# Attention and MLP on one core: q and k of the first groups transposed in 128-wide PE steps into one PSUM bank, with few long dummy matmuls

## Chip, cores, metric

One core of one Trainium2 chip. The metric is the device time of the whole program in microseconds (us). A time is quoted as the median of several executions; a profiled execution shows a span that is about 1.8 us shorter than its time.

Names used below: PE is TensorE, PEld its weight load, DVE VectorE, ACT ScalarE, POOL GpSimd, SP SyncE. Sizes such as 64\*64 or 128\*64 in a line of PE are the rows and columns of its array that the instruction uses; the text calls this its tiling. A 128x64 step is also called half-width.

## The reference

```python
# q, k, v: (8 batches, 12 heads, 448, 64), float32
scores = q @ k.T / sqrt(64) - log(448)
attn = sigmoid(scores)                       # no softmax
x = (attn @ v) -> (8 * 448 tokens, 768)
h = x @ w_in                                 # 768 x 2048
out = gelu_tanh(h) @ w_out                   # 2048 x 768
```

The kernel computes in bf16 with float32 accumulation. It treats four heads as one "group": 3 groups to a batch, 24 in all, each of 7 "units".

## The kernel before

A small scheduler inside the program simulates the engines, decides the order of the instructions on each, and then writes out the waits. So an edit of one cost or one bank also moves instructions elsewhere. q and k of the first two batches (groups 0 to 5) are transposed on PE, later ones by DMA. The parts that matter:

```python
def make_warm():                     # dummies, meant to keep PE's clock up until q and k are there
    x, y = take_pair(plan.now)
    def fn(e):
        for _ in range(4):
            for a in range(2):
                rows = slice(64 * a, 64 * a + 64)
                r = mm(ps[0:64, (x, y)[a], 0:128], ident[rows, 0:64], ident[rows, :], start=True, stop=True)
# ...
def make_trans(t):                   # one of q, k of one group: 28 steps of 64x64, two banks
    x, y = take_pair(t)
    def fn(e):
        for j in range(NJ):          # NJ = 7
            for (a, c) in ((0, 0), (1, 1), (0, 1), (1, 0)):
                rows = slice(64 * a, 64 * a + 64)
                r = nc.tensor.transpose(ps[64*c:64*c+64, (x, y)[a], 32*j:32*j+32].bitcast(BF16),
                                        part[rows, j, c, :], ident[rows, rows])
# ... then one copy out of PSUM (DVE; for group 0 DVE and ACT share it)
# qk: 4 matmuls of 64x448 a unit, then a sigmoid on ACT (batch 0) or tanh on ACT and a scaling on DVE;
# av: 4 matmuls of 64x448 a unit; MLP: 6 matmuls a tile with w_in, gelu on ACT, 16 with w_out
EARLY = "v0 q2 v1 v2 q3 v3 w0 w1 q4 v4 w2 q5 v5 w3 o0 o1 o2 o3"   # order of the loads that POOL issues
```

In EARLY, q2 means "k and q of group 2", w0 to w3 the quarters of w_in, o0 to o3 those of w_out.

Of the kernel before, what the change touches and what calls it, by code (L numbers as in the profile page):

```python
# [12 lines left out]
BF16 = mybir.dt.bfloat16  # L13
# [29 lines left out]
        self.clock = None  # L43


class Plan:


# [32 lines left out]
        return True  # L81

    def begin(self, op, t):
        op.deps = [d() if callable(d) else d for d in op.deps]
        cost = op.cost
        if op.eng == "PE":
            t0 = t
            if op.mode != self.pe_mode and self.pe_mode is not None:
                t0 = t + self.SWITCH
            self.pe_mode = op.mode  # L90
            op.start = t0
            self.free["PE"] = t0 + cost
            op.end = t0 + cost + op.lat
        elif op.eng in QUEUES:
            op.start = t
            self.free[op.eng] = float("inf") if op.hold else t + cost
            if op.hold:
                self.blocker = op
            go = t + cost * 0.5 + self.DMA_HEAD[op.eng] + (0.0 if self.order[op.eng] else self.DMA_FIRST[op.eng])
            self.flow[op.eng].append([op, float(op.pkt[0]), go])  # L100
            heapq.heappush(self.events, go)
            self.dma_count[op.sem] = self.dma_count.get(op.sem, 0) + 16
            op.target = self.dma_count[op.sem]
        else:
            op.start = t
            self.free[op.eng] = t + cost
            op.end = t + op.lat
        op.pos = len(self.order[op.eng])
        self.order[op.eng].append(op)
        if op.end is not None:  # L110
            heapq.heappush(self.events, op.end)
        if self.free[op.eng] != float("inf"):
            heapq.heappush(self.events, self.free[op.eng])
# [153 lines left out]
def bass_sigmoid_attention__then__act_gelu_tanh_kernel(  # L267
# [8 lines left out]
    B, H, S, D = q.shape  # L276
    assert D == 64 and H % 4 == 0 and S % 64 == 0 and B % 2 == 0
    NJ = S // 64
    NG = H // 4
# [25 lines left out]
    with contextlib.ExitStack() as stack:  # L305
# [26 lines left out]
        def copy(e, o, i, who):  # L332
            if who == "ACT":
                return e.activation(o, i, AF.Copy)  # L334
            return e.tensor_copy(o, i)  # L335
# [23 lines left out]
        def take(t):  # L359
            ok = [i for i in range(NPS) if bank_ok(i, t)]  # L360
            lone = [i for i in ok if not bank_ok(i ^ 1, t)]
            i = (lone or ok)[0]
            bank_busy[i] = True
            return i

        def take_pair(t):
            i = [i for i in range(0, NPS, 2) if bank_ok(i, t) and bank_ok(i + 1, t)][0]
            bank_busy[i] = bank_busy[i + 1] = True
            return i, i + 1

        def free_pairs(t):
            return sum(1 for i in range(0, NPS, 2) if bank_ok(i, t) and bank_ok(i + 1, t))
# [4 lines left out]
        def give(i, op):  # L377
            bank_free[i] = op
            bank_busy[i] = False

        def make_warm():

            x, y = take_pair(plan.now)
            prev = [bank_free[x], bank_free[y]]

            def fn(e):
                r = None
                for _ in range(4):
                    for a in range(2):
                        rows = slice(64 * a, 64 * a + 64)  # L390
                        r = mm(ps[0:64, (x, y)[a], 0:128], ident[rows, 0:64], ident[rows, :],  # L391
                               start=True, stop=True)
                return r

            op = Op("warm", "PE", fn, [eye] + prev, 235.0 if plan.now > 5500.0 else 450.0, 165.0, mode=64)
            give(x, op)
            give(y, op)
            return op


        G = B * NG
        units = [(g, j) for g in range(G) for j in range(NJ)]
        cast_q, cast_k, tr_q, tr_k, ld_q, ld_k, ld_v = {}, {}, {}, {}, {}, {}, {}
        tr_too = []
        freed_q, freed_k = {}, {}
        qk, tanh, aff, av, evac = {}, {}, {}, {}, {}
        trans = []
# [14 lines left out]
        def low_load(nm, g):  # L422

            return 2 <= g < PE_TR * NG
# [80 lines left out]
                                               prio=(1, g), sem="tr%s%d" % (nm, st), pkt=(112, 26.0), hold=0.6))  # L505

        def trans_ready(t):
            if not trans or eye.end is None or eye.end > t or free_pairs(t) < 1:
                return False
            g, nm, src, dst, cast, tr, freed, after = trans[0]  # L510
            return g in cast and cast[g].end is not None and cast[g].end <= t

        def make_trans(t):
            g, nm, src, dst, cast, tr, freed, after = trans.pop(0)
            x, y = take_pair(t)
            prev = [bank_free[x], bank_free[y]]
            flat = src[:].rearrange("p j c d -> p (j c d)")
            part = flat.rearrange("p (j c d) -> p j c d", j=NJ, c=2) if not low_load(nm, g) else \
                flat.rearrange("p (c j d) -> p j c d", c=2, j=NJ)
            to = ps[:, x:y + 1, 0:NJ * 32].bitcast(BF16)  # L520

            def fn(e):
                r = None
                for j in range(NJ):
                    for (a, c) in ((0, 0), (1, 1), (0, 1), (1, 0)):
                        rows = slice(64 * a, 64 * a + 64)
                        r = nc.tensor.transpose(ps[64 * c:64 * c + 64, (x, y)[a], 32 * j:32 * j + 32].bitcast(BF16),
                                                part[rows, j, c, :], ident[rows, rows])
                return r

            freed[g] = op = Op("trp%s%d" % (nm, g), "PE", fn, [eye, cast[g]] + prev, NJ * 70.0, 165.0, mode=64)
            o = dst[:].rearrange("p j x -> p (j x)").rearrange("p (a y) -> p a y", a=2)
            if g == 0:
                two = [plan.add(Op("trc%s%d.%d" % (nm, g, a), w,
                                   lambda e, a=a, w=w: copy(e, o[:, a], to[:, a], w),
                                   [op], 330.0, 450.0, prio=(0, -1))) for a, w in ((0, "DVE"), (1, "ACT"))]
                tr[g] = two[0]
                tr_too.extend(two[1:])
                give(x, two[0])
                give(y, two[1])  # L540
                return op
            tr[g] = plan.add(Op("trc%s%d" % (nm, g), "ANY",
                                lambda e, who: copy(e, o, to, who),
                                [op] + after, 0, 0, prio=(0, g),
                                alts={"DVE": (560.0, 680.0)}))
            give(x, tr[g])
            give(y, tr[g])
            return op

        def by_half(t, g):  # L550

            if g < PE_TR * NG:
                return t[:].rearrange("p j x -> p (j x)").rearrange("p (a j r) -> p a j r", a=2, j=NJ)
            return t[:].rearrange("p j (a r) -> p a j r", a=2)

        def make_qk(n, t):
# [4 lines left out]
            x, y = take_pair(t)  # L561
            prev = [bank_free[x], bank_free[y]]
            both = ps[:, x:y + 1, 0:S]
            kv, qv = by_half(kT[s], g), by_half(qT[s], g)

            def fn(e):
                r = None
                for (a, c, half) in ((0, 0, 0), (0, 1, 1), (1, 1, 0), (1, 0, 1)):
# [3 lines left out]
                           start=True, stop=True)  # L572
                return r

            qk[(g, j)] = op = Op("qk%d.%d" % (g, j), "PE", fn, [tr_q[g], tr_k[g]] + (tr_too if g == 0 else []) + prev,
                                 4 * 2.5 + S / 2.4, 165.0, mode=64)
            pg, pj = units[n - NAT] if n >= NAT else (None, None)
            old = av[pg] if pg is not None else None
# [243 lines left out]
        def qk_ready(t, n):  # L822
            if n >= len(units):
                return False
            g, j = units[n]
            if g not in tr_q or n >= NAT and units[n - NAT][0] not in av:
                return False
            return all(d.end is not None and d.end <= t for d in [tr_q[g], tr_k[g]] + tr_too)

        def units_done(g, t):  # L830

# [35 lines left out]
        def pe_next(pl, t):  # L867
# [8 lines left out]
            go_a, go_b = a_ready(t), b_ready(t)  # L876
            mlp = go_a or go_b
            banks = free_banks(t)
            if trans_ready(t) and mlp:
                g, nm = trans[0][:2]  # L880
                both = [x for x in trans[:2] if x[0] == g]
                if free_pairs(t) >= len(both) and all(x[4][g].end is not None and x[4][g].end <= t for x in both):
                    ops = [make_trans(t) for x in both]
                    state["queue"] = ops[1:]
                    return ops[0]
            can = 0
            if n <= LEAD + UB * 0.5 * (a_prog + b_prog):
                while can < BURST and qk_ready(t, n + can):
# [4 lines left out]
            if not mlp:  # L893
                if can and left <= 1 and free_pairs(t) and banks >= (2 if av_open else 4):
                    op = make_qk(n, t)
                    state["n"] += 1
                    return op
                soon = trans_ready(t) and trans[0][0] <= units[min(n + 3, len(units) - 1)][0]
                if m and not soon:
                    return av_take(1, t)[0]  # L900
                return make_trans(t) if trans_ready(t) and free_pairs(t) >= (1 if soon or not 0 < n < UB else 2) else None
            whole = m > 0 and state["avj"] + m == NJ
            room = (banks - (2 if whole and not av_open else 0)) // 2
            size = min(can, room, free_pairs(t))
# [121 lines left out]
```

## Time and profile before

| | before |
|---|---|
| time, median of the first 3 runs | 396.77 us (395.6 to 396.88) |
| span of the profiled run, its mean granted clock | 394.7 us, 0.995 |
| PE busy | 382.2 us, 97% |
| chain that ended last | 86% PE |

Three parts of the page: the engines' busy time in 40 equal slices (about 10 us each; a digit is tenths), the granted clock of PE, and the shares of the chain that ended last.

```profile
PE   7779999999999999999999999999999999999996
ACT  5988974377779757777657666567657733333211
PEclk9989999999999999999999999999999999999999
DMA  8999999539698566588667548727211011111133
...
PE 86%; DMA 6%; ACT 4%; DVE 1%; SPq 1%; issue 1%; POOL 0%
```

Read: PE is full from the fourth slice to the end. Only the first three slices have room, and in the second and third ACT is fuller than PE (9 and 8 against 7). The third slice has a clock of 0.8.

The next fence is PE's timeline in that slice, then ACT's. Columns: start, time, engine, line, operation, output and inputs, sizes, count; in brackets the idle time before it and what ended it.

```profile
22.34 0.36 PE L617 MATMUL ps<-at,vb 64*64 64x448 bf16 x4
22.86 0.38 PE L527 MATMUL ps<-ident,qb 64*64 64x64 bf16 x22 [0.17 <-DVE kT L335]
25.10 0.25 PE L527 MATMUL ps<-ident,qb 64*64 64x64 bf16 x6 [1.86 <-issue]
25.16 0.38 PE L570 MATMUL ps<-qT,kT 64*64 64x448 bf16 x4
```

```profile
20.30 3.39 ACT L581 ACTIVATE at<-ps 128x896 bf16<-128x896 f32 x4
25.59 1.73 ACT L581 ACTIVATE at<-ps 128x896 bf16<-128x896 f32 x2 [1.89 <-PE ps L570]
```

In the middle of one transpose, after 22 of 28 equal steps whose data and banks were all there, PE stops for 1.86 us and the profile knows no releaser ("issue"). ACT, the busiest engine of this stage, then waits 1.89 us for the qk behind it. In the next fence the stretches of 1 us show PE's clock after that stop: the column after the engines' busy times is PEclk, the last two are the DMA share and GB/s.

```profile
23.00:24.00 1.00, 0.24 (x22) 0.13 (x17) 0.00 (x0) 0.69 (x1) 1.00 (x3) 1.00 1.22 197
24.00:25.00 1.00, 0.00 (x0) 0.00 (x0) 0.00 (x0) 0.00 (x0) 1.00 (x2) 1.00 1.25 202
...
27.00:28.00 1.00, 1.00 (x16) 0.22 (x8) 0.00 (x0) 1.00 (x2) 1.00 (x2) 0.50 1.26 201
```

### The profile page before, as it was taken

How to read it: one execution, taken by the hardware profiler on the slowest of the kernel's cores; microseconds unless marked ns; L12 is line 12 of the kernel's file. 1: busy time of each engine (PE TensorE's matmuls, PEld its weight loads, DVE VectorE, ACT ScalarE, POOL GpSimd, SP SyncE). 2: the span in 40 equal slices, each digit the busy share in tenths (PEclk: the TensorE clock that was granted, in tenths of full speed). 3: DMA queues.
4: the chain of work that ended last, by engine and by line, in shares of the span. 5: the costliest groups of instructions: out<-in, count | busy, mean ns of one | idle time of the engine just before them, and what ended most of it. 6: DMA issues, size and time to landing. Idle time of an engine off the chain costs nothing.

```text
span 394.7 us, 7961 instructions
## 1 busy us (share of the span) xinstructions
PE 382.2 (97%) x3456; PEld 199.1 (50%) x3456; DVE 134.7 (34%) x226; ACT 243.3 (62%) x382; POOL 51.2 (13%) x82
## 2 busy tenths in 40 slices
PE   7779999999999999999999999999999999999996
PEld 6324445555544554554554555545554555555563
DVE  3336633036546524554434443343333210000000
ACT  5988974377779757777657666567657733333211
POOL 6992110011102010201110101101000000000000
PEclk9989999999999999999999999999999999999999
DMA  8999999539698566588667548727211011111133
GB/s 237 192 200 204 210 213 319 89 72 184 172 206 193 135 128 163 141 181 178 164 132 177 138 77 169 174 64 181 65 40 42 0 42 42 40 40 42 40 81 80
DMA packets 63523, 51.77 MB, mean 131 GB/s; under 512 B 36224, under 2 KB 60032, under 8 KB 63488
## 3 DMA queue, kind: packets, MB, share of 16 engines
q1 hardware_dynamic: 48320, 36.61, 37.6%
q0 software_dynamic: 14528, 13.64, 21.9%
q10 hardware_dynamic: 640, 1.02, 0.7%
q8 instruction: 27, 0.44, 0.4%
q14 instruction: 8, 0.07, 0.0%
HBM read 45.61 MB, written 11.01 MB: 143 GB/s over the span
## 4 chain that ended last, share of the span: by engine, by line
PE 86%; DMA 6%; ACT 4%; DVE 1%; SPq 1%; issue 1%; POOL 0%
PE ps L721 35%; PE ps L662 34%; PE ps L570 8%; PE ps L617 7%; DMA qf<-in_q_dram 4%; ACT at L581 3%; DMA vb<-in_v_dram 1%; DMA kf<-in_k_dram 1%; ACT th L589 1%; DVE at L593 1%; SPq L755 1%; ACT gT L694 0%; PE ps L676 0%; DVE qb L335 0%; DVE kT L335 0%
## 5 line engine op out<-in xcount | busy, mean ns | idle before, releaser
L662 PE MATMUL ps<-xT,w_in 128*128 128x448 bf16 x762 | 154.4, 353 | 0.4 <-DVE kT L335 0.2
L721 PE MATMUL ps<-w_out,gT 128*128 128x384 bf16 x896 | 153.1, 326 | 0.0
L593 DVE TENSOR_SCALAR at<-th 128x896 bf16<-128x896 f32 x147 | 92.4, 628 | 140.6 <-ACT th L589 140.1
L589 ACT ACTIVATE th<-ps 128x896 f32<-128x896 f32 x147 | 129.1, 927 | 1.0 <-PE ps L570 1.0
L721 PEld LDWEIGHTS ps<-w_out,gT 128*128 128x128 bf16 x896 | 86.2, 98 | 63.3 <-ACT th L589 2.9
L662 PEld LDWEIGHTS ps<-xT,w_in 128*128 128x128 bf16 x762 | 71.1, 98 | 76.7 <-ACT th L589 3.9
L694 ACT ACTIVATE gT<-ps 128x448 bf16<-128x448 f32 x128 | 71.2, 556 | 43.2 <-PE ps L662 43.2
L334 ACT ACTIVATE ob<-ps 128x384 f32<-128x384 f32 x56 | 27.5, 490 | 95.4 <-PE ps L721 95.4
L570 PE MATMUL ps<-qT,kT 64*64 64x448 bf16 x672 | 47.7, 362 | 3.8 <-ACT at L581 2.9
L466 POOL DMA_DIRECT2D vb<-in_v_dram x24 | 14.8, 617 | 217.4 <-PE ps L570 214.5
L617 PE MATMUL ps<-at,vb 64*64 64x448 bf16 x672 | 39.8, 353 | 0.8 <-DMA vb<-in_v_dram 0.8
L570 PEld LDWEIGHTS ps<-qT,kT 64*64 64x64 bf16 x672 | 14.8, 105 | 31.5 <-issue 15.9
L617 PEld LDWEIGHTS ps<-at,vb 64*64 64x64 bf16 x672 | 19.8, 107 | 12.0 <-DMA vb<-in_v_dram 1.1
L335 DVE CAST xT<-ps 128x448 bf16<-128x448 f32 x26 | 15.8, 619 | 11.7 <-PE ps L617 11.7
L581 ACT ACTIVATE at<-ps 128x896 bf16<-128x896 f32 x21 | 17.3, 949 | 2.7 <-PE ps L570 2.7
L335 DVE CAST kb<-kf 128x896 bf16<-128x896 f32 (+1 forms) x21 | 13.1, 623 | 14.2 <-DMA kf<-in_k_dram 14.2
L468 POOL DMA_DIRECT2D vb<-in_v_dram x24 | 17.6, 733 | 0.2 <-issue 0.2
L335 DVE CAST qb<-qf 128x896 bf16<-128x896 f32 x19 | 11.9, 625 | 9.8 <-DMA qf<-in_q_dram 9.8
L334 ACT ACTIVATE xT<-ps 128x448 bf16<-128x448 f32 x22 | 12.2, 560 | 2.5 <-PE ps L617 2.3
L776 POOL DMA_DIRECT2D w_in<-in_moe_w_in_dram x16 | 9.9, 652 | 0.0
L391 PE MATMUL ps<-ident 64*64 64x128 bf16 x112 | 5.5, 277 | 1.8 <-POOL ident L342 1.5
L391 PEld LDWEIGHTS ps<-ident 64*64 64x64 bf16 x112 | 5.1, 150 | 1.9 <-POOL ident L342 1.5
(27 smaller groups left out, 33.8 us busy)
## 6 DMA issues: line engine op xcount, KB each, us to landing
out_dram<-ob SPq DMA_DIRECT2D x54, 192.0 KB, 2.7
kf<-in_k_dram SPq DMA_DIRECT2D x19, 448.0 KB, 4.6
qf<-in_q_dram SPq DMA_DIRECT2D x18, 448.0 KB, 5.6
vb<-in_v_dram POOLq DMA_DIRECT2D x48, 112.0 KB, 5.2
w_in<-in_moe_w_in_dram POOLq DMA_DIRECT2D x16, 192.0 KB, 10.9
w_out<-in_moe_w_out_dram POOLq DMA_DIRECT2D x4, 768.0 KB, 22.3
kb<-in_k_dram POOLq DMA_DIRECT2D x4, 224.0 KB, 8.9
qb<-in_q_dram POOLq DMA_DIRECT2D x4, 224.0 KB, 9.4
```

The source lines that it names most:

```text
L334: return e.activation(o, i, AF.Copy)
L335: return e.tensor_copy(o, i)
L466: a = plan.add(Op("ldv%da" % g, "SWQ", lambda e, d=dst[0:64], ap=lo: e.dma_start(d, ap), deps, 610.0, 0.0, prio=order_v(g), sem="ldv%da" % ...
L468: c = plan.add(Op("ldv%db" % g, "SWQ", lambda e, d=dst[64:128], ap=hi: e.dma_start(d, ap), deps, 610.0, 0.0, prio=order_v(g), sem="ldv%db" ...
L570: r = mm(ps[64 * half:64 * half + 64, (x, y)[a], 0:S], kv[d, a, j, :], qv[d, a, :, :], start=True, stop=True)
L581: lambda e: e.activation(at[as_][:], both, AF.Sigmoid, bias=bias, scale=scale),
L589: lambda e: e.activation(th[ts][:], both, AF.Tanh, bias=0.5 * bias, scale=0.5 * scale),
L593: lambda e: e.tensor_scalar(at[as_][:], th[ts][:], 0.5, 0.5, op0=ALU.mult, op1=ALU.add),
L617: r = mm(ps[64 * c:64 * c + 64, banks[a], 0:S], vb[s][d, slot, j, :], at[as_][d, a, :], start=(j == 0), stop=(j == NJ - 1))
L662: r = mm(ps[:, bank, 0:S], w_in[:, kt, fc * 128:(fc + 1) * 128], xT[xb][:, kt, :], start=(kt == 0), stop=(kt == KT - 1))
L694: lambda e: e.activation(gT[:, fc, col:col + S], ps[:, bank, 0:S], AF.Gelu_apprx_tanh),
L721: r = mm(ps[:, bank, 0:EH], gT[:, fc, col:col + 128], w_out[:, fc, half * EH:(half + 1) * EH], start=(fc == 0), stop=(fc == FC - 1))
```

## The change

The intent, as the diff shows it: fewer PE instructions for the transposes, one PSUM bank instead of two, and a clock kept up by few long dummies.

- Groups 0 and 1: 7 full 128x128 transposes instead of 28 of 64x64. Groups 2 to 5, whose data lie otherwise in SBUF: 14 of 128x64. All of one q or k go into one bank (two for group 0, whose copy DVE and ACT share).
- Dummies: 14 matmuls of 512 columns on a zeroed tile instead of 112 of 128 columns.
- In the MLP stage, one q or k may be transposed at a time, and only while PE is in a full-height tiling. (Left out of the cut below: the scheduler also asks for other numbers of free banks before it transposes early.)

```diff
         def make_warm():
-            x, y = take_pair(plan.now)
+            bank = take(plan.now)
             def fn(e):
-                for _ in range(4):
-                    for a in range(2):
-                        ... mm(ps[0:64, (x, y)[a], 0:128], ident[rows, 0:64], ident[rows, :], ...)
+                return mm(ps[:, bank, :], ident[:], gT[:, 0, 0:512], start=True, stop=True)
 ...
         def make_trans(t):
-            x, y = take_pair(t)
+            banks = list(take_pair(t)) if g == 0 else [take(t)]
             def fn(e):
                 for j in range(NJ):
-                    for (a, c) in ((0, 0), (1, 1), (0, 1), (1, 0)):
-                        ... transpose(64 x 64)
+                    o = to[j // cut][:, 128 * j:128 * j + 128]
+                    if not low:
+                        r = nc.tensor.transpose(o, flat[:, 128 * j:128 * j + 128], ident[:])
+                        continue
+                    for c in range(2):
+                        r = nc.tensor.transpose(o[64*c:64*c+64, :], flat[:, (c*NJ+j)*D:(c*NJ+j+1)*D], ident[:])
 ...
-            if trans_ready(t) and mlp:
-                ... both of a group, if two pairs of banks are free
+            if trans_ready(t) and mlp and pl.pe_mode in (128, 12864):
+                return make_trans(t)
```

More of the change, by code (lines that the diff above doesn't have):

```diff
@@ L43, in __init__, with end @@
         self.clock = None
+class All:
+    def __init__(self, ops):
+        self.ops = ops
+    @property
+    def end(self):
+        ends = [op.end for op in self.ops]
+        return None if None in ends else max(ends)
 class Plan:
@@ L83, in begin @@
     def begin(self, op, t):
-        op.deps = [d() if callable(d) else d for d in op.deps]
+        deps = [d() if callable(d) else d for d in op.deps]
+        op.deps = [x for d in deps for x in (d.ops if isinstance(d, All) else [d])]
         cost = op.cost
@@ L379, in give @@
             bank_busy[i] = False
+        blank = plan.add(Op("blank", "DVE", lambda e: e.memset(gT[:, 0, 0:512], 0.0), [], 200.0, 300.0, prio=(0, -2)))
         def make_warm():
-            x, y = take_pair(plan.now)
-            prev = [bank_free[x], bank_free[y]]
+            bank = take(plan.now)
             def fn(e):
-                r = None
-                for _ in range(4):
-                    for a in range(2):
-                        rows = slice(64 * a, 64 * a + 64)
-                        r = mm(ps[0:64, (x, y)[a], 0:128], ident[rows, 0:64], ident[rows, :],
-                               start=True, stop=True)
-                return r
-            op = Op("warm", "PE", fn, [eye] + prev, 235.0 if plan.now > 5500.0 else 450.0, 165.0, mode=64)
-            give(x, op)
-            give(y, op)
+                return mm(ps[:, bank, :], ident[:], gT[:, 0, 0:512], start=True, stop=True)
+            op = Op("warm", "PE", fn, [eye, blank, bank_free[bank]], 225.0 if plan.now > 5500.0 else 435.0, 165.0, mode=128)
+            give(bank, op)
             return op
@@ L403, in bass_sigmoid_attention__then__act_gelu_tanh_kernel @@
         cast_q, cast_k, tr_q, tr_k, ld_q, ld_k, ld_v = {}, {}, {}, {}, {}, {}, {}
-        tr_too = []
         freed_q, freed_k = {}, {}
@@ L507, in trans_ready @@
         def trans_ready(t):
-            if not trans or eye.end is None or eye.end > t or free_pairs(t) < 1:
+            if not trans or eye.end is None or eye.end > t or free_banks(t) < 1:
+                return False
+            if trans[0][0] == 0 and not free_pairs(t):
                 return False
@@ L514, in make_trans @@
             g, nm, src, dst, cast, tr, freed, after = trans.pop(0)
-            x, y = take_pair(t)
-            prev = [bank_free[x], bank_free[y]]
+            banks = list(take_pair(t)) if g == 0 else [take(t)]
+            prev = [bank_free[x] for x in banks]
             flat = src[:].rearrange("p j c d -> p (j c d)")
-            part = flat.rearrange("p (j c d) -> p j c d", j=NJ, c=2) if not low_load(nm, g) else \
-                flat.rearrange("p (c j d) -> p j c d", c=2, j=NJ)
-            to = ps[:, x:y + 1, 0:NJ * 32].bitcast(BF16)
+            to = [ps[:, x, 0:NJ * 64].bitcast(BF16) for x in banks]
+            cut = NJ // 2 + 1 if g == 0 else NJ
+            low = low_load(nm, g)
             def fn(e):
@@ L524, in fn @@
                 for j in range(NJ):
-                    for (a, c) in ((0, 0), (1, 1), (0, 1), (1, 0)):
-                        rows = slice(64 * a, 64 * a + 64)
-                        r = nc.tensor.transpose(ps[64 * c:64 * c + 64, (x, y)[a], 32 * j:32 * j + 32].bitcast(BF16),
-                                                part[rows, j, c, :], ident[rows, rows])
-                return r
-            freed[g] = op = Op("trp%s%d" % (nm, g), "PE", fn, [eye, cast[g]] + prev, NJ * 70.0, 165.0, mode=64)
@@ L532, in make_trans @@
-            o = dst[:].rearrange("p j x -> p (j x)").rearrange("p (a y) -> p a y", a=2)
+                    o = to[j // cut][:, 128 * j:128 * j + 128]
[3 more added lines that the diff above has]
+                    for c in range(2):
+                        r = nc.tensor.transpose(o[64 * c:64 * c + 64, :], flat[:, (c * NJ + j) * D:(c * NJ + j + 1) * D],
+                                                ident[:])
@@ L533, in make_trans @@
+                return r
+            freed[g] = op = Op("trp%s%d" % (nm, g), "PE", fn, [eye, cast[g]] + prev, NJ * 56.0, 165.0, mode=12864 if low else 128)
+            flat_o = dst[:].rearrange("p j x -> p (j x)")
             if g == 0:
-                two = [plan.add(Op("trc%s%d.%d" % (nm, g, a), w,
-                                   lambda e, a=a, w=w: copy(e, o[:, a], to[:, a], w),
-                                   [op], 330.0, 450.0, prio=(0, -1))) for a, w in ((0, "DVE"), (1, "ACT"))]
@@ L537, in make_trans @@
-                tr[g] = two[0]
-                tr_too.extend(two[1:])
-                give(x, two[0])
-                give(y, two[1])
+                two = []
+                for x, (lo, hi, w) in enumerate(((0, cut * 128, "DVE"), (cut * 128, NJ * 128, "ACT"))):
+                    two.append(plan.add(Op("trc%s%d.%d" % (nm, g, x), w,
+                                           lambda e, x=x, lo=lo, hi=hi, w=w: copy(e, flat_o[:, lo:hi], to[x][:, lo:hi], w),
+                                           [op], 330.0, 450.0, prio=(0, -1))))
+                    give(banks[x], two[x])
@@ L541, in make_trans @@
+                tr[g] = All(two)
                 return op
             tr[g] = plan.add(Op("trc%s%d" % (nm, g), "ANY",
-                                lambda e, who: copy(e, o, to, who),
+                                lambda e, who: copy(e, flat_o, to[0], who),
                                 [op] + after, 0, 0, prio=(0, g),
                                 alts={"DVE": (560.0, 680.0)}))
-            give(x, tr[g])
-            give(y, tr[g])
-            return op
-        def by_half(t, g):
-            if g < PE_TR * NG:
-                return t[:].rearrange("p j x -> p (j x)").rearrange("p (a j r) -> p a j r", a=2, j=NJ)
+            give(banks[0], tr[g])
@@ L554, in by_half @@
+            return op
+        def by_half(t):
             return t[:].rearrange("p j (a r) -> p a j r", a=2)
@@ L563, in make_qk @@
             both = ps[:, x:y + 1, 0:S]
-            kv, qv = by_half(kT[s], g), by_half(qT[s], g)
+            kv, qv = by_half(kT[s]), by_half(qT[s])
             def fn(e):
@@ L573, in fn @@
                 return r
-            qk[(g, j)] = op = Op("qk%d.%d" % (g, j), "PE", fn, [tr_q[g], tr_k[g]] + (tr_too if g == 0 else []) + prev,
+            qk[(g, j)] = op = Op("qk%d.%d" % (g, j), "PE", fn, [tr_q[g], tr_k[g]] + prev,
                                  4 * 2.5 + S / 2.4, 165.0, mode=64)
@@ L827, in qk_ready @@
                 return False
-            return all(d.end is not None and d.end <= t for d in [tr_q[g], tr_k[g]] + tr_too)
+            return all(d.end is not None and d.end <= t for d in (tr_q[g], tr_k[g]))
         def units_done(g, t):
@@ L878, in pe_next @@
             banks = free_banks(t)
-            if trans_ready(t) and mlp:
-                g, nm = trans[0][:2]
-                both = [x for x in trans[:2] if x[0] == g]
-                if free_pairs(t) >= len(both) and all(x[4][g].end is not None and x[4][g].end <= t for x in both):
-                    ops = [make_trans(t) for x in both]
-                    state["queue"] = ops[1:]
-                    return ops[0]
+            if trans_ready(t) and mlp and pl.pe_mode in (128, 12864):
+                return make_trans(t)
             can = 0
@@ L900, in pe_next @@
                     return av_take(1, t)[0]
-                return make_trans(t) if trans_ready(t) and free_pairs(t) >= (1 if soon or not 0 < n < UB else 2) else None
+                return make_trans(t) if trans_ready(t) and banks >= (1 if soon or not 0 < n < UB else 3) else None
             whole = m > 0 and state["avj"] + m == NJ
```

## The prediction

> **What bounds the kernel now.** The chain that ended last is 86% PE. In the timeline PE is busy from about 30 us to the end and never waits over 0.4 us at once. Before that: until 7.8 us loads, casts, PE transposes of group 0 (5.81 to 6.4), copies, first qk; from 7.8 to 27.2 us ACT is the limit, 21 sigmoids at one each 0.82 us; at 28.3 us the first MLP matmul. So only the start, and PE work after 28 us, can move the time.
>
> In the middle of the transposes of group 3's q, PE stands still from 23.24 to 25.10 us ("issue"), and ACT then waits 1.89 us for qk. A 16 KB packet of the instruction queue was fetched at about 22.9 to 23.8 us: I read this as PE out of instructions. The granted clock is 0.50 from 26.1 to 29.5 us after it. [...]
>
> **What the change does.**
> - Twelve transposes of 28 64x64 steps, 0.22 to 0.24 us each, become 7 full steps (4 times) or 14 half-width ones (8 times). [...] 0.39 us each by estimate: +0.16 us, 1.9 us in all, plus changes of tiling beside the 64x64 qk. No run here shows that step yet.
> - 112 dummies become 14, 336 transposes 140: 294 matmuls and as many weight loads go, over two instruction blocks, all in the first 40 us.
> - Copies (DVE 0.62 us) stay. Group 4 is transposed right after the first MLP tile, 20 matmuls earlier than before.
>
> **How much is on the critical path.**
> - Group 0: transposes 0.16 us longer each, dummies at half clock: first sigmoid at about 8.1 us (+0.25). ACT then loses its 0.26 us gap at 10.4, which pays it back.
> - Groups 1 to 3 lie in PE's slack under ACT (0.24 us idle in 0.82): free.
> - Groups 4 and 5 are PE-bound: 4 x 0.16 plus switches, +0.8 us.
> - The stall should go, as 128 matmuls now last 10 us instead of 6: sigmoids end 1.9 us earlier, without a half-clock window after (up to 0.9 us more).
> - But not all is kept. Group 4's q lands at about 29.7 us, group 5's at about 37.0 us (issues 18.14 and 23.22 plus 11.6 and 13.8 to landing), and PE works in order: it waits there. Counting the work ahead, PE leaves group 5's transposes at about 37.4 us with slightly more done, where it left them at 37.98: 0.5 to 0.8 us ahead, the transposes' cost included. Nothing later changes.
>
> **Prediction.** 0.8 us under the median of 396.77: 396.0 us, 8 in 10 within 394.2 to 397.9. Faster by over 2%: 1%; within 2%: 97%; slower: 2%.
>
> **What would show it.** Transposes at about 0.4 us; first sigmoid near 8.1 us; no "issue" time over 1 us on PE near 23 us; clock 1.00 from 26 to 30 us; first MLP matmul near 26.5 us; PE waiting for the q loads of groups 4 and 5 near 29.7 and 37 us; PE without a gap from 40 us.
>
> **What would make it wrong.** The stall moves into the PE-bound part (+1 to 2 us), or was there in few of the timed runs (+0.3); half-width steps don't overlap in pairs (+1.6 us on groups 4 and 5); the clock falls to half because PE idles more between 8 and 26 us; the loads land earlier than I think (up to 2 us faster).

The sum came to 0.8 us under 396.77, 396.0 us. What the traces show for the terms:

- Block: the stops found below lie after 705 and 961 PE instructions, 256 apart, which is 128 matmuls with their weight loads. In the kernel before, those between the two counts last 5.8 us (17.26 to 23.05 us); in the changed kernel, 8.9 us from 193 to 449 (13.62 to 22.54 us) and 12.3 us from 449 to 705: the "10 us instead of 6" of the text.
- Wide transpose, 0.39 us: seven steps of 56 ns. The last dummies of the kernel before, of 128 columns, start in pairs 55 to 57 ns apart from 5.43 to 5.77 us; until 5.36 us it was 106 to 108 ns, the half clock of the text. The two of a pair start 1 to 3 ns apart there.
- Change of tiling: in the kernel before, a qk matmul starts 282 ns after the w_in matmul ahead of it, where the next w_in matmul starts after 189: an estimate of 0.09 us for a change.
- PE in order: in the changed kernel PE waited 0.61 us for group 4's q and started nothing else meanwhile.
- Clock and idle time: in the kernel before the clock was 0.50 from 25.87 to 29.28 us, after the stop of 1.86 us. The last section has what else the traces show of it.

## The result

| | before | changed |
|---|---|---|
| time, median of 6 runs | 396.14 us (395.60 to 396.88) | 395.00 us (394.32 to 395.82) |
| ratio, 95% interval | | 0.9969 (0.9952 to 0.9986) |
| span of the profiled run, mean clock | 394.7 us, 0.995 | 393.0 us, 0.999 |

The change saves about 1.2 us, 0.3%: inside the range predicted, a little more than the 0.8 us named. The range, 394.2 to 397.9 us, also held no change at all and twice the saving, so lying inside it says little; the marks in the trace say more.

The same parts of the page of the changed kernel:

```profile
PE   7779999999999999999999999999999999999996
ACT  5998964477778767767657666576647632333211
PEclk9999999999999999999999999999999999999999
...
PE 92%; DMA 4%; POOL 3%; ACT 0%; issue 0%
```

The clock has no dip in the third slice any more. PE's timeline at the place of the stop (group 3's k and q, then qk), and ACT's there:

```profile
22.13 0.58 PE L539 MATMUL ps<-ident,kb 128*64 128x128 bf16 x14
22.54 0.56 PE L539 MATMUL ps<-ident,qb 128*64 128x128 bf16 x14
23.03 0.38 PE L579 MATMUL ps<-qT,kT 64*64 64x448 bf16 x4
```

```profile
20.81 5.19 ACT L590 ACTIVATE at<-ps 128x896 bf16<-128x896 f32 x6
```

The stop is gone; ACT runs all sigmoids in one piece, six of them in this window. A transpose of q or k takes PE 0.41 us from its start to the next (22.13 to 22.54), where 28 small steps took about 0.23 us (21.62 to 21.85 in the kernel before). Further on in PE's timeline, the first MLP tile and group 4:

```profile
26.56 0.93 PE L685 MATMUL ps<-xT,w_in 128*128 128x448 bf16 x4
27.89 0.55 PE L691 MATMUL ps<-xT,w_in 128*128 128x448 bf16 x2 [0.40 <-DVE xT L348]
28.49 0.58 PE L539 MATMUL ps<-ident,kb 128*64 128x128 bf16 x14
29.68 0.58 PE L539 MATMUL ps<-ident,qb 128*64 128x128 bf16 x14 [0.61 <-DMA qb<-in_q_dram]
```

The first MLP matmul starts 1.7 us earlier than in the kernel before, whose lines for it and for the qk after group 5's transposes are:

```profile
28.29 1.40 PE L676 MATMUL ps<-xT,w_in 128*128 128x448 bf16 x4
...
38.55 0.38 PE L570 MATMUL ps<-qT,kT 64*64 64x448 bf16 x4 [0.37 <-ACT gT L694]
```

In the changed kernel PE then waits 0.61 us for the load of group 4's q: a part of the gain ends here.

The groups of transposes, before and after (line, engine, operation, names, sizes, count; busy time and mean ns of one; idle time before):

```profile
L527 PE MATMUL ps<-ident,qb 64*64 64x64 bf16 x168 | 2.7, 194 | 2.2 <-issue 1.9 <-DVE kT L335 0.3
L527 PE MATMUL ps<-ident,kb 64*64 64x64 bf16 x168 | 2.5, 195 | 0.0
```

```profile
L539 PE MATMUL ps<-ident,kb 128*64 128x128 bf16 x56 | 2.3, 223 | 0.0
L539 PE MATMUL ps<-ident,qb 128*64 128x128 bf16 x56 | 2.3, 220 | 0.6 <-DMA qb<-in_q_dram 0.6
L536 PE MATMUL ps<-ident,kb 128*128 128x128 bf16 x14 | 1.2, 230 | 0.0
L536 PE MATMUL ps<-ident,qb 128*128 128x128 bf16 x14 | 1.1, 219 | 0.0
```

336 steps became 140, but their busy time rose from 5.2 to 6.9 us.

**A running account.** Both kernels do the same useful matmuls. Give each its steady start-to-start time in the traces (0.189 us with w_in, 0.1625 with w_out, 0.0475 for qk and av), add these up in order, and subtract the sum from the clock time at which PE gets there. What is left is everything that was not useful matmul: start, waits, transposes, changes of tiling. It is my arithmetic from the traces' start times, taken at the first matmul that starts with that much work done. The third and fifth columns are second traces, of runs below: before_again1 of the kernel before, after_again of the changed one.

```
us of useful    time spent on all else, us
work done       before   before_again1   changed   after_again
     5           13.95        14.23        14.45       14.22
     9           20.50        18.78        18.77       18.55
    10           20.74        19.02        20.83       19.69
    13           22.04        20.35        21.06       19.92
    18           23.66        22.44        22.45       21.42
    60           25.42        24.20        24.14       23.14
   350           36.49        34.93        34.86       33.86
```

At 9 us of work the change is 1.73 us ahead: the stop. At 10 it has spent that on the transposes of group 4, done early, and on the wait for their load. Then the kernel before pays for the same transposes and for waits on ACT and DVE (0.17, 0.19 and 0.37 us in its timeline between 33 and 39 us), and is 1.2 us behind at 18. The last 0.4 us come later, 0.34 of them at one place at 260 us, where PE waits for DVE. That is not the order's doing: the other two traces of the kernel before have the same order and no such wait.

Columns 3 and 4 meet at 18 us of work: against a run of the kernel before without the long stop the change gains nothing in these two traces. before_again1 is 0.71 us ahead at 13 us, and loses it in a wait of 0.85 us for group 5's q, which lands at 37.07 us. Column 5 is a warning: in that second trace of the changed kernel group 4's q landed at 28.39 instead of 29.64 us, PE did not wait for it, and all that follows is 1.0 us earlier. So one trace of each kernel does not settle a difference of 1 us. The experiments say why the stop comes and goes.

### The profile page after: what moved, and what is told of

The parts are those of the page before. It is cut to its first block, busy times and chain, and to the rows that moved or that the text cites. A ratio compares the mean times of both kernels' runs of the same rounds, so it can differ in the third digit from the quotient of the medians.

```text
span 393.0 us, 7381 instructions
## 1 busy us (share of the span) xinstructions
PE 382.8 (97%) x3162; PEld 197.2 (50%) x3162; DVE 135.3 (34%) x227; ACT 243.1 (62%) x382; POOL 50.7 (13%) x82
## 4 chain that ended last, share of the span: by engine, by line
PE 92%; DMA 4%; POOL 3%; ACT 0%; issue 0%
PE ps L671 38%; PE ps L730 38%; PE ps L579 9%; PE ps L626 7%; DMA qb<-in_q_dram 3%; POOL w_in L785 1%; DMA kf<-in_k_dram 1%; POOL vb L474 1%; POOL vb L472 1%; POOL kb L446 1%; PE ps L539 0%; POOL qb L446 0%; ACT ob L347 0%
## 5 line engine op out<-in xcount | busy, mean ns | idle before, releaser
L626 PE MATMUL ps<-at,vb 64*64 64x448 bf16 x672 | 38.5, 350 | 0.0
L401 PE MATMUL ps<-gT,ident 128*128 128x512 bf16 x14 | 5.7, 578 | 1.5 <-POOL ident L355 1.5
L348 DVE COPY kT<-ps 128x896 bf16<-128x896 bf16 (+1 forms) x6 | 3.5, 590 | 4.2 <-PE ps L536 2.2
```

The source lines that it names most:

```text
L348: return e.tensor_copy(o, i)
L626: r = mm(ps[64 * c:64 * c + 64, banks[a], 0:S], vb[s][d, slot, j, :], at[as_][d, a, :], start=(j == 0), stop=(j == NJ - 1))
```

## The experiments

My theory: PE ran out of instructions, because the small transposes use them up faster than they can be fetched, and the change removed the stop by needing fewer. Rivals: (A) the long dummies and the clock they hold; (B) the single bank and the order on PE that follows.

In the traces the packets of the instruction queue have start and length, so each stop can be laid beside the packet that came last before it. "Matmul n" counts PE's matmuls from the start.

```
run              packet (us)      last start before, next start after       gap
before           22.64 to 23.54   matmul 474 at 23.05, 475 at 25.10         2.05
before_again1    21.34 to 22.23   matmul 474 at 23.32, 475 at 23.80         0.47
before_again2    21.28 to 22.17   matmul 474 at 23.43, 475 at 23.62         0.20
b_longdummy      20.68 to 21.63   matmul 346 at 21.60, 347 at 23.00         1.39
```

(Gaps are taken from the nanoseconds of the trace and then rounded.)

### b_longdummy: the dummies alone

```diff
 kernel before
-            8 matmuls of 64x128 a dummy, 112 in all
+            1 matmul of 128x512 a dummy, 14 in all      (as the change has it)
```

> The kernel before with only the dummies of the change (14 long ones for 112 short ones); transposes as before. Theory (PE runs out of instructions): 98 matmuls fewer come ahead, so the block that ran out at matmul 474 of the list is cut 98 matmuls later in the order; the block before it now begins at group 2's k transposes and ends at group 3's k transposes, again about 6 us of work, so PE stands still for 1.5 to 2.5 us near 22 us, just after group 3's k transposes instead of inside its q transposes; time as before, 395.7 to 396.6 us. Rival A (the dummies, by a clock that is full earlier or steadier, made the gain): no stall, 395.0 us. Rival B (one bank, order of PE): 396.1 us and the stall still at 23.2 us inside group 3's q transposes.

Measured: 394.65 us (394.38 to 396.10, 6 runs), ratio to before 0.9975 (0.9946 to 1.0004). The time is that of rival A, and my number was wrong. But the trace does not show rival A. PE's timeline, with the lines of its weight loads (PEld) for the same qk:

```profile
21.35 0.41 PE L521 MATMUL ps<-ident,kb 64*64 64x64 bf16 x28
21.57 0.38 PE L611 MATMUL ps<-at,vb 64*64 64x448 bf16 x4
21.85 0.10 PEld L564 LDWEIGHTS ps<-qT,kT 64*64 64x64 bf16 x1 [0.17 <-ACT at L575]
23.00 0.38 PE L564 MATMUL ps<-qT,kT 64*64 64x448 bf16 x4 [1.04 <-ACT at L575]
23.00 0.11 PEld L564 LDWEIGHTS ps<-qT,kT 64*64 64x64 bf16 x3 [1.04 <-issue]
```

and ACT's:

```profile
23.43 0.92 ACT L575 ACTIVATE at<-ps 128x896 bf16<-128x896 f32 x1 [0.81 <-PE ps L564]
```

There is a stop, at the foretold place just after group 3's k transposes. The profile puts PE's 1.04 us down to ACT. But the first weight load of this same qk, which waited for ACT, ran at 21.85 us; by then ACT had released it, and what was missing until 23.00 us was the matmul behind it and the other three loads ("issue"). ACT itself ran out of work for 0.81 us, waiting for this qk. And by count of all PE instructions in the trace (matmuls, weight loads, semaphore waits) the stop stands after 705 of them, exactly 256 before the one of the kernel before, which stands after 961. It also ends 1.36 us after a packet of instructions has come. So the place follows the count of instructions, not the work. The stop was shorter than the one in the kernel before because the packet came earlier.

### b_halfdummy: half as many dummies, twice as long

```diff
 kernel before
-                for _ in range(4):          # and 128 columns
+                for _ in range(2):          # and 256 columns, on a zeroed tile
```

> The kernel before with half as many dummies of twice the length (56 matmuls instead of 112); transposes as before. Theory: block limits move by 56 matmuls, the one that was at 23.24 us falls to about 30.7 us in the list, and the one before it to about 19.7 us[...]: stall under 0.8 us or none, ACT not held up, first MLP matmul before 27.3 us; 394.9 to 395.6 us although no transpose was changed. Rival B (one bank or the order of PE made the gain): as before, 396.1 us.

Measured: 394.26 us (393.87 to 394.88), ratio 0.9960 (0.9932 to 0.9988). ACT's timeline has one piece where the kernel before has the hole:

```profile
16.20 9.14 ACT L584 ACTIVATE at<-ps 128x896 bf16<-128x896 f32 x11
```

No transpose was changed, no bank, and PE's order is the same but for one pair of steps; 56 matmuls and 56 weight loads fewer come ahead, and the stop is gone, with 2 us of the median. It was even a little faster than I wrote. By count, instructions 705 and 961, after which a new block begins, now start at 20.53 and 28.42 us (I had about 19.7 and 30.7), and PE passes both without a stop, the first just 1.57 us after its packet has come. So the gain can be had without rival B's single bank and order.

### a_pad_olddummy: as many instructions again in the changed kernel

```diff
 changed kernel, with the old 112 dummies
+                if g < 4:
+                    for x in range(28 - NJ * (2 if low else 1)):   # useless 64x64 transposes first
+                        nc.tensor.transpose(to[0][64*c:64*c+64, 0:64], flat[0:64, 0:64], ident[0:64, 0:64])
```

> The changed kernel with the old dummies and with useless 64x64 transposes ahead of those of groups 0 to 3, so that PE has as many instructions up to there as before; result unchanged, order otherwise that of the change. Theory: the stall is back, 1.5 to 2.2 us of issue time on PE near 23 us, ACT waits as long, first MLP matmul after 28 us; 396.0 to 396.8 us. Rival B (one bank, order of PE): no stall, 395.0 to 395.3 us.

Measured: 396.35 us (396.29 to 397.06), ratio 1.0015 (0.9987 to 1.0042): the time I expected, for another reason. There was no stop. The padding took PE 0.3 to 0.5 us for each q or k, more than I had counted on, so group 0 was late (the first sigmoid at 9.72 us instead of 8.33) and PE took longer over the same number of instructions. The experiment failed to make what it was to make, and says nothing about the theory.

### a_q4: group 4's loads earlier

```diff
 changed kernel
-        EARLY = "v0 q2 v1 v2 q3 v3 w0 w1 q4 v4 w2 ..."
+        EARLY = "v0 q2 v1 v2 q3 v3 w0 q4 w1 v4 w2 ..."
```

> The changed kernel with the loads of group 4's k and q issued ahead of the second quarter of w_in. Theory (the gain is cut short by the wait for these loads): the wait of 0.6 us for q of group 4 and the 0.5 us for k go; 394.0 to 394.8 us, where the change takes 395.0. Rival (that wait only hides waits for ACT and DVE that come next): 394.8 to 395.2 us, with new waits for gT or kT between 30 and 38 us.

Measured: 393.50 us (393.12 to 394.41), ratio 0.9944 (0.9913 to 0.9975), against 0.9969 and 0.9965 for the change in two sets of runs. PE now transposes group 4's k at 24.52 us, in ACT's stage, and waits 0.41 us for q at 26.02 us; the wait at 29.7 us is gone. The theory holds: the load did cut the gain. It was faster than my range said, and earlier loads were worth about 0.9 us by the ratios, though on different chips and with wide intervals.

### The kernel before has two faces

The 33 executions of the kernel before that were timed beside these experiments fall into two heaps by their mean granted clock: 9 at 0.998 or more, median 394.81 us (394.19 to 395.89), and 24 below that, median 396.70 us (394.53 to 397.95). The heaps overlap: four of the 24 took 394.53 to 395.51 us. I had the first 11 when I took this to mean that not the stop but the half-clock window after it costs the time, and tested that next.

### after_again and a_hold: a stop of another cause

after_again is the changed kernel unchanged. a_hold makes PE stop at the old place by a fill on DVE:

```diff
 changed kernel
+            if (g, nm) == (3, "k"):
+                held.append(plan.add(Op("hold", "DVE", lambda e: e.memset(gT[:, 4:9, :], 0.0), [op], ...)))
+            if (g, nm) == (3, "q"):
+                op.deps.append(held[0])
```

> The changed kernel once more, as a mate for the runs beside it on one chip. Both theories: 394.5 to 395.5 us, granted clock 0.998 or more in every run. The kernel before, timed beside it, splits by clock: 394.4 to 395.0 us in runs of 0.998 or more, 396.0 to 397.0 us in runs of 0.996 or less.

> The changed kernel, with group 3's q transposes made to wait for a fill of 2.3 us on DVE that starts when the k transposes end: PE stands still for about 2 us near 22.6 us, from another cause than instructions; same order on PE. Theory (it is the half-clock window after a stall that costs, the stall itself is swallowed by later waits for loads): more than a third of the runs have a mean clock of 0.996 or less and take 396.2 to 397.2 us, the others at 0.998 or more take 394.8 to 395.6 us. Rival (the stall itself, through the sigmoids, costs its 2 us whatever the clock): every run 396.5 to 397 us, whatever its clock. Rival 2 (only an instruction stall does it): all runs as the changed kernel, 395.0 us, clock full.

Measured: after_again 394.41 us (393.85 to 395.25), ratio 0.9965, clock 0.998 or more in all runs. The kernel before beside it split less cleanly than I wrote: two of its four runs at full clock took 395.20 and 395.88 us, and one of the seven others 395.40. a_hold 396.99 us (396.82 to 397.72), ratio 1.0031. PE's and DVE's lines show the stop:

```profile
22.35 0.58 PE L540 MATMUL ps<-ident,kb 128*64 128x128 bf16 x14
...
23.47 1.93 DVE L546 MEMSET gT<- 128x2240 uint32 x1 [1.27 <-PE ps L540]
...
25.54 0.58 PE L540 MATMUL ps<-ident,qb 128*64 128x128 bf16 x14 [2.61 <-DVE gT L546]
...
26.49 0.92 ACT L595 ACTIVATE at<-ps 128x896 bf16<-128x896 f32 x1 [2.89 <-PE ps L584]
```

The profiled run of a_hold had a clock of 1.0 and took 396.96 us; the five others had 0.995 or 0.996 and took 396.82 to 397.72. So my idea fell: a stop of 2.6 us costs 2.6 us, and whether the clock drops after it makes no difference that these runs show. The rival written beside it was right, though two of the six runs lay above its range. Then the two heaps of the kernel before must differ in the stop itself.

### a_hold1: a shorter stop

The same with `gT[:, 4:6, :]`, a fill of 0.81 us.

> As the 2.3 us hold, but with a fill of about 0.8 us: ACT should wait some 1.7 us, close to the 1.89 us of the kernel before. The 2.3 us hold cost 2.5 us at full clock and at half clock alike, so my idea that only the half-clock window costs has fallen; the theory is now that the stall itself costs nearly its length, less about 0.3 us. Then 395.5 to 396.2 us, where the changed kernel takes 394.4 to 395.0, and no split by clock. If waits for loads swallowed a stall of this size: under 395.1 us.

Measured: 395.25 us (394.95 to 395.68), clock 0.998 or more. PE waited 1.21 us and ACT 1.49 us, less than the 1.7 I had aimed at. The kernel beside it on the same chip without a hold (a_olddummy, next) took 394.55 us: the hold cost 0.7 us, under my range because the stop was smaller. So a stop at this place costs most of its length: 0.7 us of 1.21 here (the kernel beside it has other dummies, so this is rough), 2.6 of 2.61 in a_hold.

### before_again1, before_again2: the other face in a trace

The kernel before, once each, for a trace.

> The kernel before once more, for a trace. Theory now: in runs of clock 0.998 or more, near 394.5 us, the instruction stall near 23 us is short (PE gap under 1.2 us, ACT waits under 0.8 us); in runs of clock 0.996, near 396.5 us, it is about 2 us with the half-clock window after it. Rival (the stall is the same in both and the clock makes the difference): the gap is about 2 us also in a run of full clock.

> As the run ahead of it: the kernel before once more, in the hope that one of the two traces is of the full clock; the same two readings are told apart.

Measured: 394.90 and 394.89 us, both at a clock of 1.0. PE's timeline in the first, and ACT's:

```profile
23.14 0.38 PE L527 MATMUL ps<-ident,qb 64*64 64x64 bf16 x22 [0.16 <-DVE kT L335]
23.80 0.25 PE L527 MATMUL ps<-ident,qb 64*64 64x64 bf16 x6 [0.28 <-issue]
23.85 0.38 PE L570 MATMUL ps<-qT,kT 64*64 64x448 bf16 x4
```

```profile
24.28 1.73 ACT L581 ACTIVATE at<-ps 128x896 bf16<-128x896 f32 x2 [0.31 <-PE ps L570]
```

The same 22 steps, the same break before the other 6, but 0.28 us of idle time instead of 1.86. The packet of instructions had come at 22.23 us instead of 23.54 (the table above): 1.3 us earlier, as much as the break is shorter within 0.3 us. In the three runs where PE is held at the break by more than 0.4 us, it goes on 1.36 to 1.57 us after the packet. The program is the same to the last instruction; what varies is when the packet is fetched. This settles the theory, and it tells what the change is worth: against a run of the kernel before without the long stop, nothing that these runs can show. The spans are 393.1 and 393.0 us (392.0 in after_again); the 9 full-clock runs of the kernel before have a median of 394.81 us, the 12 runs of the change 394.73. The lead that before_again1 has over the changed kernel in the traces goes at the load of group 5's q, for which it waits:

```profile
37.11 0.41 PE L527 MATMUL ps<-ident,qb 64*64 64x64 bf16 x28 [0.85 <-DMA qb<-in_q_dram]
```

### a_olddummy: the transposes of the change alone

```diff
 changed kernel
-            14 long dummies
+            112 short dummies, as before
```

> The transposes of the change alone, with the old 112 short dummies. Theory: a block limit falls at about 16 us and the next at about 24.5 us, over 8 us apart, so there is no instruction stall; as the changed kernel, 394.4 to 395.4 us, clock full in every run. Rival (long dummies are needed for the gain): 396 us with runs at a clock of 0.996.

Measured: 394.55 us (393.80 to 395.06), ratio 0.9953 (0.9926 to 0.9981), clock 1.0 in all runs. As expected; the limits (instructions 449 and 705) fell at 16.04 and 23.32 us. So the dummies alone shorten the stop, the transposes alone remove it, and both together do no better than one. The long dummies of rival A are not needed. By this account what counts is how fast PE uses up the block of instructions that falls on the transposes of groups 2 and 3.

### a_tr64 and a_q4_tr64: small steps where PE is the limit

```diff
 changed kernel
-            groups 4 and 5: 14 steps of 128x64, one bank
+            groups 4 and 5: 28 steps of 64x64, two banks, as before
 (a_q4_tr64: and q4 ahead of w1 in EARLY)
```

> The changed kernel with groups 4 and 5 transposed as before, in 28 64x64 steps and two banks; groups 0 to 3 and the dummies as changed. Theory (the wide steps cost the PE-bound part 0.18 us each of four and two changes of tiling): 0.4 to 0.9 us under the changed kernel, near 394.4 us, clock full. Rival (wide steps are free, one bank is a gain): 395.0 us or slower.

> The same with group 4's loads also issued ahead of the second quarter of w_in. Theory: both gains add where the wait for q of group 4 is gone: 392.7 to 393.5 us, 1.5 to 2.3 us under the changed kernel. Rival (the earlier loads only move the wait): 394.0 to 394.5 us.

Measured: a_tr64 393.38 us (393.01 to 394.46), ratio 0.9941 (0.9917 to 0.9965), 1.0 us under after_again on the same chip. PE's timeline at group 4:

```profile
28.38 0.41 PE L550 MATMUL ps<-ident,kb 64*64 64x64 bf16 x28
28.62 0.36 PE L596 MATMUL ps<-qT,kT 64*64 64x448 bf16 x4
28.91 1.31 PE L688 MATMUL ps<-xT,w_in 128*128 128x448 bf16 x6
30.15 0.41 PE L550 MATMUL ps<-ident,qb 64*64 64x64 bf16 x28
```

Each takes 0.24 us instead of 0.41. The small steps share the tiling of qk, so the scheduler puts them next to it, and q comes late enough not to wait for its load. The gain is above my range of 0.4 to 0.9 us. Against the first trace of the changed kernel part of it would be the load. Against after_again, where PE does not wait for that load either, the profiled spans differ by 0.5 us (391.5 and 392.0): close to the four times 0.17 us that the wide steps take longer, though of one trace each.

a_q4_tr64 took 394.15 us (393.53 to 395.49), not the 392.7 to 393.5 expected. It is further ahead at first, and then meets the next load, in PE's timeline:

```profile
56.47 2.76 PE L747 MATMUL ps<-w_out,gT 128*128 128x384 bf16 x16 [0.78 <-DMA w_out<-in_moe_w_out_dram]
```

The scheduler, believing in a faster load of w_out, put the first matmul that needs it earlier, after 96 matmuls with w_in where the other versions do 126. Here the rival was right: the wait moved. a_tr64 and a_q4 are the fastest versions, within 0.2 us of each other; the intervals do not part them.

## Why the prediction was right

- **What bounds it, and where the change can act:** right. PE is full after 30 us in both traces, and the transposes of groups 1 to 3 were free under ACT.
- **The stop is PE out of instructions, and goes:** right, and shown together by b_longdummy (it comes exactly 256 instructions earlier, after 705 instead of 961, at other work), b_halfdummy (it goes without any new transpose) and the two further traces of the kernel before (same place, length set by the packet).
- **Cost of a wide transpose 0.39 us:** 0.41 us measured. First sigmoid at 8.1 us: 8.33, of which about 0.16 us is a later landing of k. First MLP matmul near 26.5 us: 26.56. Clock 1.00 from 26 to 30 us: yes.
- **Group 4's q holds PE at 29.7 us:** right in the trace shown (29.68 us), not in after_again, where it landed at 28.39 us. **Group 5's q holds it at 37 us:** wrong, by little; it landed at 36.91 us and PE began it at 37.16 us without a wait. In before_again1 it did hold PE, until 37.11 us.
- **0.5 to 0.8 us ahead after group 5's transposes:** right. At the last step of these the changed kernel stands at 37.50 us with 0.19 us more of useful work done, the kernel before at 37.98 us: 0.67 us ahead.
- **"Nothing later changes", and with it the size, 0.8 us:** wrong. By the account of the two first traces the lead is 1.2 us at 18 us of work (about 41 us of time) and 1.6 us at the end. The kernel before loses 0.37 us right after group 5's transposes in a wait for a gelu, which stood in the trace that the prediction was made from, and 0.34 us at 260 us, which its other traces do not lose.
- **The stop as a constant of the kernel before:** my sum took one trace as the kernel. It was a face that about 20 to 24 of 33 further runs show, judged by time and clock; only three of its runs were traced. The mean gain of 1.2 to 1.4 us is a mixture: about 2 us against those runs, about nothing against the others. The prediction named "was there in few of the timed runs" as a way to be wrong; it was there in most. That the mean of this mixture lies near the 0.8 us named is in part luck: the sum was of one stalled trace, whose own gain in the traces is 1.6 us.
- **The half-clock window "up to 0.9 us more":** not seen. a_hold took the same time with and without it. My later idea that it explains all was wrong too.

A slip without consequence: the times of the packet and of the half clock in the prediction were read with a zero that was 0.24 us off; they are 22.64 to 23.54 and 25.87 to 29.28 us.

Open: why the packet comes 1.3 us later in some runs. POOL issued loads without a pause in both. The loads are late too: group 3's k and q land at 16.74 and 17.84 us in the first trace, at 15.73 and 17.01 us in before_again1, before the packet that comes late. This fits a longer backlog of DMA work in that run as the reason, but it is not shown; an experiment with fewer loads in that stage was not made.

## What to carry to other kernels

Where PE runs many tiny instructions while the DMA queues are full (here 128 matmuls in 5.8 us at a DMA share of 1.2), look for idle time of kind "issue" in the middle of a run of equal steps, and count the PE instructions between such places: here the stops lay 256 apart (705 and 961), which pointed to instructions as the limit. A change of their number ahead of it, also in places that cost no time themselves, moved the limits along the work: this removed the stop in b_halfdummy and moved it in b_longdummy. Before crediting a change with a gain, look whether the kernel before has two faces; one trace may show the worse one. What was gained in the stage before the bottleneck was kept only up to the next load that PE had to wait for (0.61 us for group 4's q in the changed kernel, 0.85 us for group 5's in before_again1), so move that load too, and check what the scheduler then runs into.

## What the traces show of instruction fetch, steps and clock

- Instruction fetch: the packets of the instruction queue hold 16 KB (27 packets, 0.44 MB in the kernel before), and the stops come after 961 and 705 PE instructions, 256 apart. At the two limits before it, after instructions 449 and 705 of the kernel before, there is no stop: the next instruction starts 0.15 and 0.04 us later, and 0.15 us also lies between a qk and the av behind it just ahead of the first. After 961 there is one: gaps of 0.20 to 2.05 us in three traces, where 128 matmuls had lasted about 6 us (5.8 in the first) while POOL issued loads without a pause. From the packet's end to PE going on it took 1.36 to 1.57 us in the three runs held longest.
- The stop after 961 PE instructions ends after a packet whose fetch began 0.4 us before it (22.64 against 23.05 us). How many instructions PE holds ready is not shown.
- Steps: in the changed kernel the seven 128x128 steps of a transpose start 55 to 57 ns apart at most places, and took 0.40 us from their start to the next transpose (9.62 to 10.02 us); 14 half-width ones took 0.41 us and start in pairs, 2 to 4 ns apart in a pair and then 52 to 53 ns, so these overlap in pairs.
- Clock: in the kernel before it fell to 0.50 for 3.41 us after a stop of 1.86 us; in the profiled run of a_hold it did not fall after a stop of 2.6 us. The traces suggest why. In all 14 of them the first rise of the clock and its fall at the end lie 113 or 114 times 3.413 us apart. On that grid (an estimate), PE was idle for 2.03 of the 3.41 us before the fall at 25.87 us, while a_hold's stop is cut in two, with 1.46 and 1.76 us idle in the two windows; no other window from the first rise on, up to the last before the fall at the end, has more than 1.76. How much idle time in a window is enough is not shown.
